# Attention and MLP in one instruction order: filler ordered by a clock, one exponential for two heads, fp32 maxima, and ScalarE for half of the second MLP product

## The chip, the cores and the metric

The kernel runs on one core of a Trainium2 chip. The metric is the device time in microseconds of one execution. The profile is of one execution of its own, with its own time. Engines: PE is TensorE's matmul and PEld its weight load, DVE is VectorE, ACT is ScalarE, POOL is GpSimd, SP is SyncE, which issues all DMAs here.

## The reference

```python
def _A_ref(x, wqkv, wo):              # 32 heads of 20, window of 256
    qkv = (x @ wqkv).reshape(B, S, 3, H, Dh).transpose(2, 0, 3, 1, 4)
    q, k, v = qkv[0], qkv[1], qkv[2]
    scores = jnp.einsum("bhqd,bhkd->bhqk", q, k) * (Dh ** -0.5)
    mask = (idx[:, None] - idx[None, :] >= 0) & (idx[:, None] - idx[None, :] < W)
    p = _softmax(jnp.where(mask[None, None], scores, -1e9), axis=-1)
    o = jnp.einsum("bhqk,bhkd->bhqd", p, v)
    return o.transpose(0, 2, 1, 3).reshape(B, S, D) @ wo
def _B_ref(x, w1, b1, w2, b2):
    h = jnp.einsum("bsd,df->bsf", x, w1) + b1
    r = jnp.where(h > 0, h, 0)
    return jnp.einsum("bsf,fd->bsd", r * r, w2) + b2
xn = _layernorm(A_x)
return A_x + _A_ref(xn, A_wqkv, A_wo) * _silu(_B_ref(xn, B_w1, B_b1, B_w2, B_b2))
```

x is 2048 x 640, wqkv 640 x 1920, w1 640 x 1536, w2 1536 x 640, wo 640 x 640, all fp32.

## The kernel before

Every fp32 operand of a product is split into a high part, rounded to the format in which PE multiplies, and a low part that is the rest; a product is high by high, high by low and low by high, summed in PSUM. So what leaves PSUM for a further product is copied by ACT (the high part) and subtracted by DVE or POOL (the low part).

**Before the loop** x is normalized, transposed and split (`transpose_chunks`, `split`, L111 to L113), the first q and k groups and all of v are computed, and q, k and v are stored in DRAM.

**The loop** (from L1149 on) has 268 steps: 16 pairs of heads by 16 query tiles, and 12 steps of lag. In step s:

- `scores` (L485): the scores of query tile q against its three key tiles, one matmul per head, into tile `sps`. `maxima` (L497) is a DVE reduction per head that adds the mask and takes the row maximum (`junk`, `mt`, L503). After four query tiles DVE splits the maxima into two bf16 parts (`mp`, L507 and L508).
- `scores_t` (L535), 9 steps behind: the transposed scores of key tile kb against three query tiles, with two more rows of `qs` that hold the negated maxima, into `stps`. `exps` (L546) is one ACT exponential per head (L549), and POOL zeroes the masked ends (L550, L552).
- `max_rows` (L511), in every fourth step: PE transposes the split maxima (L520) into the unused last quarter of the `sps` banks, DVE copies them to `mrow` (L526), and two DMAs bring them into the rows of `qs`.
- `high` (L555) and `low` (L560): the exponentials as two fp16 parts, by ACT (L557) and DVE (L563).
- `values` (L570), in every second step: 24 pairs of matmuls by v (tile `ops`); `normed` divides by the sums.
- `fill`: a generator, `filler` (L873), yields after each matmul of the other products: the remaining q and k groups (`qkps`), then eight MLP blocks (two halves of the hidden layer by four token blocks; `hps`, then `yps`), then the output projection. `fill` runs it until an amount of estimated PE time is used up: 35% of a step's share ahead of `high` and `low`, the rest behind, with a swing of 0.3 us between odd and even steps.

**Halves.** A product's matmuls are cut into the upper and the lower 64 rows of the array, which run side by side. `half` (L479) issues one at L481; the front half of a job runs ahead, the back half is put between later front halves, by two clocks, `clock[0]` and `clock[1]`, that add up the costs in `COST`. L481 is therefore the line of all of `qkps`, `hps`, `yps` and `ops`.

**Banks.** PSUM has 3 banks for the filler's products (`Acc`, L659), 2 for `sps`, 2 for `stps`, 1 for `ops`. An `Acc` takes the bank that was freed first, in program order; PE then waits for that bank's last reader.

**Evacuations.** When a job's back half is done, its evacuation is put into `pending`, and `soon` emits it once the clock is 0.3 us further (`SOON`); `flush` in the middle of each step emits all. For `hps`, `part` (L949 to L957) takes half of a bank: ACT's relu and square, DVE's `sq`, POOL's low part; the second half comes later, from the list `late`. For `yps` (L990) DVE adds b2 (first half of the hidden layer) or the stored first sum `yin` (second half), and `ysb` goes to DRAM.

**Weights** come in pieces: a DMA to `raw`, then ACT's high and DVE's low part (L812, L815), handed out by `tick` in the middle of a step.

All engines run in the order in which the program emits (`manual_schedule`); the semaphores are put in by the framework. Behind the loop, `out_filler` transposes the attention's output (`otp`), multiplies by wo (`wops`) and joins the two branches.

Of the kernel before, what the change touches and what calls it, by code (L numbers as in the profile page):

```python
# [16 lines left out]
P = 128  # L17
# [22 lines left out]
EARLY_FILL = 0.35  # L40
SWING = 0.3
# [9 lines left out]
SOON = 0.3  # L51
# [7 lines left out]
def attn_mlp_kernel(ctx: ExitStack, tc, x, wqkv, wo, w1, b1, w2, b2, out):  # L59
# [5 lines left out]
    pat = ctx.enter_context(tc.tile_pool(name="pat", bufs=2, space=PSUM))  # L65
    po_ = ctx.enter_context(tc.tile_pool(name="po", bufs=1, space=PSUM))
    turn = [0]
# [24 lines left out]
    identb = const.tile([P, P], BF16, name="identb")  # L92
    nc.gpsimd.tensor_copy(identb, ident)
# [5 lines left out]
    mps = [const.tile([P, P], BF16, name=f"mp{i}") for i in range(2)]  # L99
    for t_ in mps:  # L100
        nc.gpsimd.memset(t_, 0.0)
# [35 lines left out]
    with tc.tile_pool(name="ph1v", bufs=2) as p1v, tc.tile_pool(name="ph1", bufs=2) as p1, tc.tile_pool(name="ph1x", bufs=4) as p1b, tc.tile_pool(name="ph1w", bufs=1) as p1w:  # L137
# [34 lines left out]
        def transpose_chunks(b, xns):  # L172
            for c in range(KC):
                ps = mm_bank([P, BT], "tps") if c % 3 == 0 else pat.tile([P, BT], F32, tag=("s", "st")[c % 3 - 1], name="tps")
# [100 lines left out]
        with tc.manual_schedule(engines={E_.PE, E_.Activation, E_.DVE, E_.Pool, E_.SP}):  # L275
# [30 lines left out]
            def turned(t):  # L306
                nc.vector.reciprocal(rstd[:, t:t + 1], rstd[:, t:t + 1])
                xn = normalize(xts[0][t], mv[:, t, :], rstd[:, t:t + 1])
                r = []
                for c0, c1 in ((0, 4), (4, 5)):  # L310
                    ps = mm_bank([P, c1 - c0, P], "tps") if c0 == 0 else pat.tile([P, c1 - c0, P], F32, tag="s", name="tps")
# [17 lines left out]
            def first_group(w):  # L329
                firsts.append((w, 0, pat.tile([P, BT // 2], F32, tag="st", name="qkps"), 0, BT // 2))  # L330
                qk_group(*firsts[-1])
# [34 lines left out]
            for w in "kq":  # L366
                ps = pat.tile([P, BT // 2], F32, tag="s", name="qkps")
                seconds.append((w, 0, ps, BT // 2, BT // 2))
                qk_group(*seconds[-1])
# [113 lines left out]
    mts = {}  # L483

    def scores(p, q):  # L485
        i = p % 2
        k0 = max(0, q - 2)
        nk = (q - k0 + 1) * P
        r = [pat.tile([P, 4 * P], F32, tag="s", name="sps") for _ in range(2)]

        def one(hh):
            o = slice(hh * HP, hh * HP + KR)
            nc.tensor.matmul(r[hh][:, :nk], qs[i][o, q * P:(q + 1) * P], ks[i][o, k0 * P:k0 * P + nk], start=True, stop=True)  # L493
        both(lambda: one(0), lambda: one(1), COST[nk])
        return r, nk

    def maxima(p, q, r, nk):  # L497
        if q % 4 == 0:
            mts[p, q // 4] = at2.tile([P, 2, 4], F32, tag="mt", name="mt")
        mt = mts[p, q // 4]  # L500
        for hh in range(2):
            junk = at2.tile([P, 3 * P], BF16, tag="junk", name="junk")
            nc.vector.tensor_tensor_reduce(out=junk[:, :nk], in0=r[hh][:, :nk], in1=mask[:, 3 * P - nk:], scale=1.0, scalar=-3.0e38, op0=ALU.add, op1=ALU.max, accum_out=mt[:, hh, q % 4:q % 4 + 1])  # L503
        if q % 4 == 3:

            mp = mps[q // 4 % 2][:, 0:16].rearrange("p (h a b) -> p h a b", h=2, a=2)
            nc.vector.tensor_scalar(mp[:, :, 0, :], mt, -1.0, None, ALU.mult)  # L507
            nc.vector.scalar_tensor_tensor(mp[:, :, 1, :], mt, -1.0, mp[:, :, 0, :], ALU.mult, ALU.subtract)  # L508
            mts[p, q // 4] = mps[q // 4 % 2]

    def max_rows(p, g, tps=None):  # L511
        i = p % 2
        mp = mts.pop((p, g))
        if tps is None:
            tps = [pat.tile([P, 4 * P], F32, tag="s", name="mtp") for _ in range(2)]
        tps = [t_[:, 3 * P:3 * P + HP // 2].bitcast(BF16) for t_ in tps]

        def one(j):
            r = slice(j * HP, (j + 1) * HP)
            nc.tensor.transpose(tps[j], mp[r, :], identb[r, r])  # L520
        both(lambda: one(0), lambda: one(1), COST[61])

        def rest():
            mrow = at2.tile([16, P], F32R, tag="mrow", name="mrow")
            for j in range(2):
                nc.vector.tensor_copy(mrow[:, j * HP:(j + 1) * HP], tps[j][0:16, :])  # L526
# [8 lines left out]
    def scores_t(p, kb):  # L535
        i = p % 2
        n = min(3, NT - kb) * P
        r = [pat.tile([P, 3 * P], F32, tag="st", name="stps") for _ in range(2)]

        def one(hh):  # L540
            o = slice(hh * HP, hh * HP + KR + 2)
            nc.tensor.matmul(r[hh][:, :n], ks[i][o, kb * P:(kb + 1) * P], qs[i][o, kb * P:kb * P + n], start=True, stop=True)  # L542
        both(lambda: one(0), lambda: one(1), COST[n])
        return r, n

    def exps(p, kb, r, n):  # L546
        p32 = at2.tile([P, 2, 3 * P], F32, tag="p32", bufs=3, name="p32")
        for hh in range(2):
            nc.scalar.activation(p32[:, hh, :n], r[hh][:, :n], AF.Exp, scale=SCALE, bias=ebias)  # L549
# [82 lines left out]
    ended = deque()  # L632
    halved = [0.0]

    def soon():
        now = clock[0]
        if late and now >= halved[0] + 2 * SOON:
            flush(flushed[0])
        if ended and now >= ended[0][1] + SOON:
            flush(ended.popleft()[0])  # L640

    def flush(upto=None):
        halved[0] = clock[0]
# [13 lines left out]
    banks = [0, 1, 2]  # L657

    class Acc:  # L659

        def __init__(self, n, name):
# [211 lines left out]
    def filler():  # L873
# [5 lines left out]
        for g, b in order_qk:  # L879
# [9 lines left out]
            for w in "qk":  # L889
                hi, lo = (t() for t in ws[g][w])  # L890
                ps = Acc(BT, "qkps")

                def evac(ps=ps, w=w, g=g, b=b):
# [4 lines left out]
                    ps.free()  # L898
# [20 lines left out]
        for n, (hf, b) in enumerate(blocks):  # L919
# [11 lines left out]
            hs, whole, nxt = {}, set(), []  # L931
# [8 lines left out]
            for th in range(2):  # L940
                for fp in range(NFH // 2):
                    ps = Acc(BT, "hps")

                    def evac(ps=ps, th=th, fp=fp, fi=hf * NFH + 2 * fp, hs=hs, whole=whole):
# [31 lines left out]
            for tt in range(4):  # L976
# [4 lines left out]
                def start(nh, hf=hf, t=t, place=place, idx=4 * (n - NB) + tt, end=n == NB - 1 and tt == 3, n=n, tt=tt):  # L981
# [3 lines left out]
                    def evac():  # L985
# [4 lines left out]
                        nc.vector.tensor_add(ysb[:, sl], ps.tile, (yins[t] if hf else b2t)[:, sl])  # L990
                        ps.free()
# [21 lines left out]
                for nh in range(2):  # L1013
                    job = start(nh)
# [12 lines left out]
        ensure("o")  # L1027
        yield from out_filler(wo_part)
# [3 lines left out]
    def ready(u):  # L1032
        return state[2] >= NP * NT - NT + 4 * (u // 2) + 3 + LAG + 5
# [25 lines left out]
    def out_filler(wo_part):  # L1059
# [6 lines left out]
        def transposes(u):  # L1066
            ob = ld[u][0]
            big = bigp.tile([P, KC * BT], F32R, tag="big", name=f"oT_{u}")
            oT[u] = big.rearrange("p (s c n) -> p s c n", s=2, c=KC)
            for c0 in range(0, KC, 2):  # L1070
# [4 lines left out]
                else:  # L1075
                    ps = pat.tile([P, len(cs), MT], F32, tag="st" if c0 == 2 else "s", name="otp")
# [48 lines left out]

    fl = filler()
# [14 lines left out]
    per = total / (steps - 1)  # L1141
    with tc.manual_schedule(engines={E_.PE, E_.Activation, E_.DVE, E_.Pool, E_.SP}):
# [6 lines left out]
        for s in range(steps):  # L1149
# [17 lines left out]
            rows = between = None  # L1167
            if s % 4 == 0 and 0 < s <= NP * NT:
                def between(tps=None, s=s):
                    return max_rows((s - 1) // NT, (s - 1) % NT // 4, tps)  # L1170
# [4 lines left out]
            if between:  # L1175
                rows = between(sc[0] if a else None)
            if a:
                maxima(*a, *sc)
# [4 lines left out]
            if b:  # L1183
                exs[b] = (exps(*b, *stp), stp[1])
            fill(EARLY_FILL * per)
# [52 lines left out]
```

## Time and profile before

| | us |
|---|---|
| median of 3 runs (lowest to highest) | 956.03 (954.85 to 958.91) |
| the profiled execution | 955.41 |
| its span, first to last instruction | 953.7 |
| mean granted TensorE clock | 0.991 |

The page gives busy shares of the span; a busy PE isn't PE at its peak, since two halves may run side by side or one alone. A row of a group has its line, engine, operation, tiles (out<-in), shape and count, then busy us and mean ns of one, then the idle time of the engine just before and what ended it. A row of waits has us in total, times and the longest.

### The profile page before, as it was taken

What the parts mean: (1) busy time and instruction counts of PE and PEld (TensorE: products, weight loads), DVE (VectorE), ACT (ScalarE), POOL (GpSimd) and SP (SyncE); (2) the same over time, 40 slices, a digit from 0 to 9 for tenths busy, and PEclk for the clock granted to TensorE, in tenths of its full rate; (3) what the DMA queues carried; (4) which work ended last, traced back from release to release, by engine and by line L of the source; (5) the groups of instructions that cost most, each with busy time, mean ns of one, the idle gap of its engine ahead of it and who ended that gap; (6) DMA issues with size and microseconds to landing.
All of it is one profiled execution on the core that took longest, in us unless ns stands there. A gap on an engine that the chain in (4) does not pass through costs nothing.

```text
span 953.7 us, 35554 instructions
## 1 busy us (share of the span) xinstructions
PE 898.4 (94%) x14368; PEld 850.3 (89%) x14368; DVE 757.3 (79%) x2085; ACT 648.0 (68%) x1240; POOL 507.4 (53%) x800
## 2 busy tenths in 40 slices
PE   8999999999999989999999889889989989989998
PEld 8999989998888889889899879789889989888998
DVE  7774378998999988878888889978888878864564
ACT  4444347887778967867968867967877967873231
POOL 5010004665556866766867756856776856761000
PEclk9999999999999999999999999999999999999999
DMA  7997788787686262354355244465265274054773
GB/s 250 285 399 276 233 258 255 223 253 252 202 262 193 70 208 85 75 195 112 80 187 147 73 139 121 112 190 151 73 195 156 52 221 124 10 191 142 268 284 126
DMA packets 106108, 169.95 MB, mean 178 GB/s; under 512 B 42072, under 2 KB 59608, under 8 KB 103384
## 3 DMA queue, kind: packets, MB, share of 16 engines
q1 hardware_dynamic: 105944, 167.68, 56.1%
q8 instruction: 113, 1.85, 0.9%
q14 instruction: 51, 0.42, 0.2%
HBM read 96.15 MB, written 70.91 MB: 175 GB/s over the span
## 4 chain that ended last, share of the span: by engine, by line
PE 59%; DVE 20%; ACT 12%; issue 6%; POOL 3%; DMA 0%; DVEq 0%; ACTq 0%; POOLq 0%
PE yps L481 14%; PE ops L481 8%; PE wops L654 7%; PE vps L232 7%; PE qkps L481 6%; DVE junk L503 6%; DVE pl L563 5%; ACT p L549 5%; PE hps L481 5%; PE sps L493 4%; DVE sq L956 3%; PE qkps L209 3%; PE stps L542 3%; ACT relu L953 2%; ACT ph L557 2%
## 5 line engine op out<-in xcount | busy, mean ns | idle before, releaser
L549 ACT ACTIVATE p<-stps,ebias 128x384 f32<-128x384 f32 (+2 forms) x512 | 258.5, 557 | 140.7 <-PE stps L542 62.2
L481 PE MATMUL yps<-w,hh 64*128 64x320 f32 x1536 | 256.9, 320 | 35.1 <-DVE sq L956 24.1
L503 DVE CUSTOM_DVE_ANT_0 junk<-sps,mask 128x384 bf16<-128x384 f32 (+2 forms) x512 | 250.3, 525 | 46.9 <-PE sps L493 30.0
L550 POOL TENSOR_SCALAR_AFFINE_SELECT p<-p 128x256 f32<-128x256 f32 x256 | 151.0, 590 | 234.4 <-ACT p L549 160.6
L563 DVE TENSOR_TENSOR pl<-p,ph 128x768 f16<-128x768 f32 (+2 forms) x256 | 247.8, 968 | 3.5 <-ACT p L549 2.3
L481 PE MATMUL hps<-xb,w 64*128 64x256 f32 x2520 | 236.5, 285 | 2.5 <-DVE ysb L990 2.5
L481 PEld LDWEIGHTS yps<-w,hh 64*128 64x128 f32 x1536 | 197.8, 190 | 43.9 <-DVE sq L956 27.8
L481 PEld LDWEIGHTS hps<-xb,w 64*128 64x128 f32 x2520 | 221.1, 187 | 4.1 <-DVE ysb L990 4.1
L557 ACT ACTIVATE ph<-p 128x768 f16<-128x768 f32 (+2 forms) x256 | 205.7, 804 | 0.0
L481 PE MATMUL ops<-vp,ph 64*128 64x61 bf16 x2880 | 203.8, 190 | 0.1
L481 PE MATMUL ops<-vp,pl 64*128 64x61 bf16 x2880 | 201.7, 189 | 0.0
L481 PE MATMUL yps<-w,hl 64*128 64x320 f32 x768 | 193.4, 320 | 0.0
L481 PEld LDWEIGHTS <-pl 64*128 64x128 f16 x2880 | 177.1, 94 | 0.1
L481 PEld LDWEIGHTS <-ph 64*128 64x128 f16 x2880 | 174.4, 94 | 2.2 <-PE stps L542 0.6
L552 POOL TENSOR_SCALAR_AFFINE_SELECT p<-p 128x256 f32<-128x256 f32 x224 | 133.6, 596 | 0.0
L493 PE MATMUL sps<-ks,qs 60*128 60x384 f32 (+2 forms) x512 | 124.7, 366 | 8.4 <-DVE mrow L526 3.7
L481 PEld LDWEIGHTS yps<-w,hl 64*128 64x128 f32 x768 | 122.9, 189 | 0.0
L542 PE MATMUL stps<-qs,ks 62*128 62x384 f32 (+2 forms) x512 | 110.7, 344 | 0.3 <-DMA qs<-mrow 0.2
L481 PE MATMUL qkps<-xT,wgkh 64*128 64x512 f32 x320 | 103.8, 400 | 0.0
L957 POOL TENSOR_TENSOR hl<-sq,hh 128x256 fp32r<-128x256 f32 x96 | 88.2, 925 | 29.0 <-DVE sq L956 23.5
L481 PE MATMUL qkps<-xT,wgqh 64*128 64x512 f32 x320 | 103.2, 399 | 0.0
L493 PEld LDWEIGHTS sps<-ks,qs 60*128 60x128 f32 x512 | 69.0, 187 | 24.3 <-DVE mt L503 15.3
(110 smaller groups left out, 1627.0 us busy)
## 6 DMA issues: line engine op xcount, KB each, us to landing
ks<-k_d SPq DMA_DIRECT2D x64, 240.0 KB
qs<-q_d SPq DMA_DIRECT2D x64, 240.0 KB
xb<-xs SPq DMA_DIRECT2D x12, 1280.0 KB
xs<-xT SPq DMA_DIRECT2D x8, 1280.0 KB
y<-ysb SPq DMA_DIRECT2D x32, 320.0 KB
k_d<-shm SPq DMA_DIRECT2D x19, 512.0 KB
q_d<-shm SPq DMA_DIRECT2D x19, 512.0 KB
v_d<-vt SPq DMA_DIRECT2D x8, 976.0 KB
```

The lines of the kernel that those rows point to most:

```text
L232: nc.tensor.matmul(ps, xT[xp][b][:, c * BT + t * P: c * BT + (t + 1) * P], wv[wp][:, c, nh * HALF:(nh + 1) * HALF], start=first and m == 0 ...
L481: return nc.tensor.matmul(out, a[r], b_[r], skip_group_check=True, **kw)
L493: nc.tensor.matmul(r[hh][:, :nk], qs[i][o, q * P:(q + 1) * P], ks[i][o, k0 * P:k0 * P + nk], start=True, stop=True)
L503: nc.vector.tensor_tensor_reduce(out=junk[:, :nk], in0=r[hh][:, :nk], in1=mask[:, 3 * P - nk:], scale=1.0, scalar=-3.0e38, op0=ALU.add, op ...
L542: nc.tensor.matmul(r[hh][:, :n], ks[i][o, kb * P:(kb + 1) * P], qs[i][o, kb * P:kb * P + n], start=True, stop=True)
L549: nc.scalar.activation(p32[:, hh, :n], r[hh][:, :n], AF.Exp, scale=SCALE, bias=ebias)
L550: nc.gpsimd.affine_select(p32[:, :, 0:P], p32[:, :, 0:P], pattern=[[0, 2], [1, P]], compare_op=ALU.is_ge, fill=0.0, base=0, channel_multip ...
L552: nc.gpsimd.affine_select(p32[:, :, 2 * P:], p32[:, :, 2 * P:], pattern=[[0, 2], [-1, P]], compare_op=ALU.is_gt, fill=0.0, base=0, channel ...
L557: nc.scalar.activation(ph[:, :, :n], p32[:, :, :n], AF.Copy)
L563: nc.vector.tensor_sub(pl[:, :, :n], p32[:, :, :n], ph[:, :, :n])
L654: nc.tensor.matmul(ps, a, b_, start=j == 0, stop=j == n - 1)
L957: nc.gpsimd.tensor_sub(hh[1][:, sl], sq, f32(hh[0][:, sl]))
```

## The change

- **Order by a clock.** `fill` runs until `clock[0]` reaches a target: 40% of a step's `pace` ahead of `high` and `low`, the whole at the step's end, less the cost of `values` where it follows. `pace` is the estimated PE time of all products and the attention's matmuls, by the step. `banks` holds with each bank the time at which it is expected free: 2.0 us after a q or k evacuation is emitted, 1.6 us after an MLP one. `room` yields the rest of the slot unless a bank is expected within `PATIENCE`, 0.5 us; a second product that lacks its input does the same. An evacuation is emitted as soon as its job is done, with the DMAs that are due ahead of it.
- **One exponential.** `sps` and `stps` become one tile of two banks each, and one ACT instruction takes both heads.
- **Maxima.** They stay fp32 in one tile `mt`, PE transposes them as fp32, and the split is made on the way out of PSUM: ACT the negated high part, DVE the rest. Four DMAs, one per head and part, in place of two.
- **b2.** In the first half of the hidden layer ACT copies `yps` out and nothing is added; b2 is added when the stored sum is read back for the output, by one DVE instruction on 128x1280 for each of eight pieces. The loads for the output begin a step later.

```diff
-EARLY_FILL = 0.35
-SWING = 0.3
+EARLY_FILL = 0.4
-SOON = 0.3
+SOON = 0.4
+PATIENCE = 0.5
...
+    spair, tpair = (pat.tile([P, 2, BT], F32, tag=t_, name=t_) for t_ in ("sps", "stps"))
+    turn, swap = [0], [0, 0]
+
+    def at_bank(k, n):
+        swap[k] ^= 1
+        return (spair, tpair)[k][:, swap[k], :n]
...
+            m = 32 * (q // 4 % 2) + 4 * hh + q % 4
+            nc.vector.tensor_tensor_reduce(out=junk[:, :nk], in0=spair[:, hh, :nk], in1=mask[:, 3 * P - nk:], scale=1.0, scalar=-3.0e38, op0=ALU.add, op1=ALU.max, accum_out=mt[:, m:m + 1])
+
+    def max_rows(p, g):
...
-            nc.tensor.transpose(tps[j], mp[r, :], identb[r, r])
-        both(lambda: one(0), lambda: one(1), COST[61])
+            nc.tensor.transpose(spair[:, j, 3 * P:3 * P + HP], mt[r, :], ident[r, r])
+        both(lambda: one(0), lambda: one(1), COST[P])
...
-            mrow = at2.tile([16, P], F32R, tag="mrow", name="mrow")
-            for j in range(2):
-                nc.vector.tensor_copy(mrow[:, j * HP:(j + 1) * HP], tps[j][0:16, :])
+            m = slice(32 * (g % 2), 32 * (g % 2) + 8)
+            mrow = at2.tile([40, 2, P], F32R, tag="mrow", bufs=1, name="mrow")[m]
+            hi, lo = (mrow[:, a, :].rearrange("m (j n) -> m j n", j=2) for a in range(2))
+            src = spair[m, :, 3 * P:3 * P + HP]
+            nc.scalar.activation(hi, src, AF.Copy, scale=-1.0)
+            nc.vector.scalar_tensor_tensor(lo, src, -1.0, f32(hi), ALU.mult, ALU.subtract)
             for hh in range(2):
-                o = hh * HP + KR
-                post(f32(qs[i])[o:o + 2, g * 512:(g + 1) * 512].rearrange("o (a n) -> o a n", a=4), f32(mrow)[8 * hh:8 * hh + 8, :])
+                for a in range(2):
+                    o = hh * HP + KR + a
+                    post(f32(qs[i])[o:o + 1, g * 512:(g + 1) * 512].rearrange("r (q n) -> r q n", q=4), f32(mrow)[4 * hh:4 * hh + 4, a, :])
...
-        for hh in range(2):
-            nc.scalar.activation(p32[:, hh, :n], r[hh][:, :n], AF.Exp, scale=SCALE, bias=ebias)
+        nc.scalar.activation(p32[:, :, :n], tpair[:, :, :n], AF.Exp, scale=SCALE, bias=ebias)
...
     def soon():
-        now = clock[0]
-        if late and now >= halved[0] + 2 * SOON:
+        if late and clock[0] >= halved[0] + SOON:
             flush(flushed[0])
-        if ended and now >= ended[0][1] + SOON:
-            flush(ended.popleft()[0])
...
-    banks = [0, 1, 2]
+    banks = [(0.0, j) for j in range(3)]
+
+    def room():
+        while state[2] < 10 ** 6 and not (banks and banks[0][0] < clock[0] + PATIENCE):
+            yield None
...
-            self.bank, self.n = banks.pop(0), n
+            (at_, self.bank), self.n = banks.pop(0), n
+            clock[0] = max(clock[0], at_)
...
-        def free(self):
-            banks.append(self.bank)
+        def free(self, after):
+            banks.append((clock[0] + after, self.bank))
+            banks.sort()
...
         def done():
-            pending.append(evac)
-            ended.append((mark(), clock[1]))
+            if state[2] < 10 ** 6:
+                flush()
+                post_all()
+                evac()
+            else:
+                pending.append(evac)
...
+                yield from room()
                 ps = Acc(BT, "qkps")
...
-                    ps.free()
+                    ps.free(2.0)
...
+                    yield from room()
                     ps = Acc(BT, "hps")
...
-                            whole.add((th, fp))
-                            ps.free()
+                            made.add((th, fp))
+                            ps.free(1.6)
                         late.append(rest)
+                        halved[0] = clock[0]
...
-                        nc.vector.tensor_add(ysb[:, sl], ps.tile, (yins[t] if hf else b2t)[:, sl])
-                        ps.free()
+                        if hf:
+                            nc.vector.tensor_add(ysb[:, sl], ps.tile, yins[t][:, sl])
+                        else:
+                            nc.scalar.activation(ysb[:, sl], ps.tile, AF.Copy)
+                        ps.free(1.6)
...
-                    while (tt // 2, fc // 2) not in whole:
-                        if pending or late:
+                    while (tt // 2, fc // 2) not in made:
+                        if state[2] < 10 ** 6:
+                            yield None
+                        elif pending or late:
                             flush()
-                            yield None
...
-        return state[2] >= NP * NT - NT + 4 * (u // 2) + 3 + LAG + 5
+        return state[2] >= NP * NT - NT + 4 * (u // 2) + 3 + LAG + 6
...
-            ob = ld[u][0]
+            ob, yb = ld[u]
+            nc.vector.tensor_add(yb, yb, b2t.unsqueeze(1).to_broadcast([P, 2, D]))
...
-    total = 8 * (KC - 1) * 15 * 0.213 + 2 * NB * (6 * 15 * 0.213 + 8 * 18 * 0.133)
     steps = NP * NT + LAG + 3
-
-    def fill(amount):
-        state[1] += amount
-        while state[0] < state[1]:
+    pace = (8 * (KC - 1) * 15 * COST[BT] + 4 * NB * (3 * 30 * COST[MT] + 4 * 18 * COST[HALF]) + NP * (2 * NT * COST[3 * P] + 12 * NT * COST[61])) / (steps - 1)
+
+    def fill(upto):
+        while clock[0] < upto:
             c = next(fl, None)
             if c is None:
-                state[1] = state[0]
+                clock[0] = upto
                 return
-            state[0] += c
+            if whole[0]:
+                clock[:2] = [clock[0] + c] * 2
...
-            fill(EARLY_FILL * per)
+            fill((s + EARLY_FILL) * pace)
...
-            fill((1 - EARLY_FILL) * per + SWING * (-1) ** (s - LAG - 3))
             if e and e[1] % 2:
+                fill((s + 1) * pace - 24 * COST[61])
                 values(*e)
+            else:
+                fill((s + 1) * pace)
```

More of the change, by code (lines that the diff above doesn't have):

```diff
@@ L366, in attn_mlp_kernel @@
             for w in "kq":
-                ps = pat.tile([P, BT // 2], F32, tag="s", name="qkps")
+                ps = at_bank(0, BT // 2)
                 seconds.append((w, 0, ps, BT // 2, BT // 2))
@@ L488, in scores @@
         nk = (q - k0 + 1) * P
-        r = [pat.tile([P, 4 * P], F32, tag="s", name="sps") for _ in range(2)]
         def one(hh):
             o = slice(hh * HP, hh * HP + KR)
-            nc.tensor.matmul(r[hh][:, :nk], qs[i][o, q * P:(q + 1) * P], ks[i][o, k0 * P:k0 * P + nk], start=True, stop=True)
+            nc.tensor.matmul(spair[:, hh, :nk], qs[i][o, q * P:(q + 1) * P], ks[i][o, k0 * P:k0 * P + nk], start=True, stop=True)
         both(lambda: one(0), lambda: one(1), COST[nk])
-        return r, nk
@@ L497, in maxima @@
[L497 to L500, printed above, removed]
+        return nk
+    def maxima(p, q, nk):
         for hh in range(2):
             junk = at2.tile([P, 3 * P], BF16, tag="junk", name="junk")
[L503 to L509, printed above, removed]
@@ L1013, in filler @@
                 for nh in range(2):
+                    yield from room()
                     job = start(nh)
@@ L1075, in transposes @@
                 else:
-                    ps = pat.tile([P, len(cs), MT], F32, tag="st" if c0 == 2 else "s", name="otp")
+                    ps = at_bank(c0 == 2, len(cs) * MT).rearrange("p (c n) -> p c n", n=MT)
                 for c in cs:
@@ L1166, in attn_mlp_kernel @@
                     load_v(p + 1)
[L1167 to L1170, printed above, removed]
+            rows = None
             if a:
@@ L1174, in attn_mlp_kernel @@
                 stp = scores_t(*b)
-            if between:
-                rows = between(sc[0] if a else None)
+            if s % 4 == 0 and 0 < s <= NP * NT:
+                rows = max_rows((s - 1) // NT, (s - 1) % NT // 4)
             if a:
-                maxima(*a, *sc)
+                maxima(*a, sc)
             if rows:
```

40 lines of the change are left out of this document (14 added, 26 removed).

## The prediction

> **What bounds the kernel now.** I read four views in this order: the page's busy shares and its chain of work that ended last, then busy time by stage, then who waited for whom, then one stall in the timeline.
>
> ```profile
> PE 898.4 (94%) x14368; PEld 850.3 (89%) x14368; DVE 757.3 (79%) x2085; ACT 648.0 (68%) x1240; POOL 507.4 (53%) x800
> ...
> PE 59%; DVE 20%; ACT 12%; issue 6%; POOL 3%; DMA 0%; DVEq 0%; ACTq 0%; POOLq 0%
> ```
>
> TensorE is busy nearly always, and yet the chain lies on it for 59% only: a third of the time something else decides. The stages tell where (columns: length, then busy time of PE, PEld, DVE, ACT, POOL, then the granted clock, DMA share and GB/s).
>
> ```profile
> 118.00:303.70 185.70, 182.51 (x2708) 165.75 (x2709) 165.85 (x481) 140.26 (x254) 96.80 (x161) 1.00 0.78 243
> 303.70:868.00 564.30, 519.65 (x10313) 494.10 (x10309) 475.16 (x1351) 436.04 (x841) 389.78 (x605) 0.98 0.44 127
> 868.00:953.70 85.70, 81.02 (x606) 80.10 (x604) 44.60 (x89) 22.03 (x34) 1.50 (x3) 1.00 0.63 216
> 506.00:526.70 20.70, 20.67 (x465) 20.21 (x460) 17.88 (x54) 18.44 (x37) 17.31 (x27) 1.00 0.40 109
> 526.70:555.00 28.30, 22.51 (x415) 21.19 (x411) 23.66 (x65) 21.39 (x43) 17.65 (x29) 0.94 0.34 89
> ```
>
> The loop of 268 steps runs from 118 to 868 us: 750 us, 2.80 a step. In its first part (the q and k products) PE hardly rests. In its second (the MLP blocks) PE idles 564.3 - 519.65 = 44.7 us. The last two rows are eight steps each, counted by their pairs of sps matmuls: the first eight take 20.7 us (2.59 a step) with PE never idle, the next eight 28.3 us with PE idle for 5.8. So the steps have a clean pace of 2.59, and stretches that fall off it.
>
> ```profile
> PE yps L481 <- DVE sq L956: 24.1, 15, 2.6
> PE yps L481 <- DVE ysb L990: 10.6, 15, 2.2
> PE sps L493 <- DVE mrow L526: 3.7, 8, 0.7
> PE sps L493 <- DVE mt L503: 3.2, 9, 1.1
> PE hps L481 <- DVE ysb L990: 2.5, 5, 0.9
> ```
>
> The rows give total us, times and the longest. 24.1 + 10.6 + 2.5 = 37.2 us of the idle time are the first matmul of an MLP accumulation that waits for a DVE reader to empty one of the three mm banks. One of them, in the timeline:
>
> ```profile
> 549.50 1.12 DVE L563 TENSOR_TENSOR pl<-p,ph 128x768 f16<-128x768 f32 x1
> 550.55 1.22 DVE L815 TENSOR_TENSOR w<-raw,w 128x512 fp32r<-128x512 f32 x2
> 551.70 0.48 DVE L990 TENSOR_TENSOR ysb<-yps,b2t 128x320 f32<-128x320 f32 x1
> 552.23 0.42 PE L481 MATMUL yps<-w,hh 64*128 64x320 f32 x1 [2.19 <-DVE ysb L990]
> 553.19 1.05 ACT L549 ACTIVATE p<-stps,ebias 128x384 f32<-128x384 f32 x2 [2.39 <-PE stps L542]
> ```
>
> DVE does a low half of the weights before the copy that frees the bank, PE stands for 2.19 us, and behind that matmul in PE's queue wait the next step's scores, for which ACT stands 2.39 us. No engine is full here: one order of instructions holds three of them. Then the clock:
>
> ```profile
> 400.00:425.00 25.00, 22.02 (x394) 20.63 (x391) 19.47 (x62) 16.74 (x32) 16.67 (x27) 0.93 0.59 191
> ...
> 825.00:850.00 25.00, 21.67 (x397) 20.56 (x392) 17.51 (x33) 20.28 (x38) 18.75 (x31) 0.93 0.22 61
> ```
>
> Five stretches of 25 us in the loop are granted 0.93, of which these are the first and the last (the others begin at 525, 550 and 625); the rest have 1.00. Each of the five has such a stall in it or just before: 5 x 25 x 0.07 = 8.7 us lost.
>
> **The change part by part.**
>
> *The order by a clock.* A product now starts only if its own clock expects a bank within 0.5 us; otherwise the filler gives up the rest of its slot and the attention matmuls come next in PE's queue. The evacuation is put in the queues of ACT and DVE as the group's last matmul is emitted, where before it stood 0.3 us of that clock behind. Giving up a slot costs PE nothing by itself, as its queue holds no pause: the work moves to a later step, at worst behind the last one. So the 37.2 us can go. They go where the guess (a bank is free 1.6 or 2.0 us after its evacuation is queued) covers DVE's backlog; above, the copy itself took 0.48 us and stood behind 2.2 us of other work, more than the guess. I take two thirds: **-24.8** (bounds 0 and -37.2). The clock follows, two thirds of 8.7: **-5.8** (0 to -8.7).
>
> The Trainium skill, "TensorE: Matmul & The Clock Gate", section "Why this matters for your kernels", has the rate fall only after idle gaps of over about 3 us. No wait above is longer than 2.6 us, so by that rule these dips aren't the stalls' doing, the term is 0 and the sum 923; its section "A second HAM failure mode: psum-queue depth-cycling" does allow for many short ones.
>
> *DVE's load.* Rows, with busy us and mean ns:
>
> ```profile
> L508 DVE SCALAR_TENSOR_TENSOR mp<-mt,mp 128x8 bf16<-128x8 f32 x64 | 13.4, 210 | 2.2
> L507 DVE TENSOR_SCALAR mp<-mt 128x8 bf16<-128x8 f32 x64 | 13.1, 205 | 2.2
> L526 DVE CAST mrow<-sps 16x64 fp32r<-16x64 bf16 x126 | 21.3, 204 | 0.0
> L503 DVE CUSTOM_DVE_ANT_0 junk<-sps,mask 128x128 bf16<-128x128 f32 x32 | 7.9, 283 | 2.6 <-PE sps L520 2.2
> L990 DVE TENSOR_TENSOR ysb<-yps,b2t 128x320 f32<-128x320 f32 x32 | 15.2, 476 | 0.2 <-PE yps L481 0.2
> L563 DVE TENSOR_TENSOR pl<-p,ph 128x768 f16<-128x768 f32 x224 | 227.5, 1015 | 3.0 <-ACT p L549 2.3 <-PE stps L542 0.5 <-ACT ph L557 0.2
> ```
>
> Gone are the two operations that split the maxima, both casts out of PSUM and the 32 additions of b2: 13.4 + 13.1 + 21.3 + 15.2 = 63.0 us. New is one subtraction of 8x128 out of PSUM for each of 64 groups, not in the trace; bounds are the cast's 204 ns and, for two operands of 128 elements, 283; I take 283, the nearer form: 18.1 us. DVE sheds 44.9 us in the loop. It is the limiter only where the chain says so, 20% of the span: **-9** (0 if it is elsewhere, -45 if DVE decided all through).
>
> *ACT.*
>
> ```profile
> L549 ACT ACTIVATE p<-stps,ebias 128x384 f32<-128x384 f32 x448 | 235.2, 578 | 119.2 <-PE stps L542 55.4 <-DVE pl L563 33.2 <-PE sps L520 25.7
> L549 ACT ACTIVATE p<-stps,ebias 128x128 f32<-128x128 f32 x32 | 10.0, 363 | 12.8 <-DVE pl L563 6.3 <-PE sps L520 5.3 <-PE ops L481 0.7
> L557 ACT ACTIVATE ph<-p 128x768 f16<-128x768 f32 x224 | 189.1, 844 | 0.0
> L256 ACT ACTIVATE vt<-vps 128x320 bf16<-128x320 f32 x32 | 14.5, 452 | 41.0 <-PE vps L232 38.7 <-DMA v_d<-vt 2.2
> ```
>
> Back to back an exponential takes 235.2 / 448 = 0.525 us, a pair 1.05. The line through 363 ns at 128 elements and 578 at 384 gives 0.90 at 768 (low bound 0.84, the copy of that size; high 1.05): 0.15 saved in each of 256 steps, 38 us. Back come 32 copies of 128x320 at 0.453 (14.5 us), and 64 copies of 8x128 out of PSUM, which the trace doesn't have: 0.36 by the 128-element exponential, bounds 0.20 (the smallest cast above, on DVE) and 0.58: 23 us. Net nothing: **0** (-16 to +11 in busy time, of which 12% is on the chain). The new wait: the negated maxima stand before the exponential in ACT's queue and wait for the transposes, which PE issues right behind the stps pair that the exponential waits for anyway. So PE's two short matmuls hide it; without that cover it would be 64 x 0.2 = 13 us on the exponentials, the high copies behind them and POOL.
>
> The Trainium skill, "ScalarE: Activation LUTs", section "Rules for kernel authors", speaks against the moved copies: plain arithmetic belongs on VectorE, up to three times as fast in bf16. This trace differs for the fp32 PSUM form, 452 ns on ACT against 476 on DVE. At three times 476 the copies would cost 31 us more of ACT, at its share of 12% +4, and the sum 921.
>
> *PE's transposes and the rows.*
>
> ```profile
> L520 PE MATMUL sps<-identb,mp 64*128 64x64 bf16 x126 | 14.0, 203 | 0.4
> ...
> 876.19 1.09 PE otp L1079 x10
> ...
> PEld L520 <- DVE mp L508: 4.0, 13, 0.8
> ...
> L623 SPq DMA_DIRECT2D qs<-mrow x128: 610/617/711, 129.3 to 832.9; - x128
> ...
> PE stps L542 <- DMA qs<-mrow: 0.2, 1, 0.2
> ```
>
> An fp32 transposition of 128 columns takes 0.109 us in the chain, one of 64 about half. In place of the bf16 pair I take +0.03 for each of 64: **+2** (0 to 64 x 0.109 = +7). The transposition no longer waits for the split maxima, 4.0 us of waits of which PE's pipeline hid some: **-2** (0 to -4). The rows go to qs in four DMAs in place of two. SP issues one in 0.62 us, so the last leaves 1.2 us later; behind it on SP stand weights, stores and the blocks' loads. The scores that need the rows come three steps (3 x 2.59 = 7.8 us) later and have waited once for 0.2 us: **0** (to +13, 0.2 for each group, if the slack is used up).
>
> *The tail.* b2 is added to 128x1280 in eight pieces: by 1015 ns for 768 elements 1.69 us each, 13.5 in all. DVE is busy for 44.6 of 85.7 us there, PE for 81.0, so all but the first lie beside PE. The first lies beside the first transposes and ACT's copy: **+1** (0 to +13.5).
>
> *Sum:* -24.8 - 5.8 - 9 - 2 + 2 + 1 = -38.6. The profiled execution took 955.41 (a span of 953.7 and 1.7 around it), 0.6 under the median of 956.03. Forecast 955.4 - 38.6 = **916.8**.
>
> **The rivals.**
>
> 1. All stalls go: every step runs at 2.59. 268 x 2.59 = 694 in place of 750, so 955.4 - 56 = 899. For it: the clean eight steps, with DVE busy for 17.88 of 20.70, show that the pace can be held through a product stage. Against: the first part is near DVE's limit (165.85 of 185.7) without any bank wait.
> 2. The stalls move: the clock that orders doesn't know DVE's backlog, so the banks still come late, or the scores wait for DVE's maxima (6.9 us now) in place of the products. Then only the lighter DVE counts: 955.4 - 9 - 2 + 3 = 947. For it: the 2.2 us of other work ahead of the copy above.
> 3. The clock dips have another cause: 916.8 + 5.8 = 923.
> 4. Slower: evacuations queued too early. ACT and DVE take their queues in order; a copy that stands ahead of its group's last matmul holds the high and low copies behind it, then `pts`, then the values on PE. There are 32 + 64 + 2 x 48 = 192 pieces. If each waits the 0.3 us that the old order allowed, 58 us come back: 916.8 + 58 = 975. It decides from 38.6 / 192 = 0.20 us a piece. For it: ACT's exponentials already wait 55.4 us for PE's stps (their row above), so ACT does run up to PE's front. Against: that is at the head of a step; inside a step, as in the stall shown, the copies come late because ACT and DVE are behind.
> 5. It does not do what it says: the clock's order comes out like the old one, and the time with it, 955.
>
> **How the numbers follow.** Forecast (900 to 936) 0.48; all stalls go (885 to 900) 0.15; the clock's other cause 0.05 (inside the first one's span); the stalls move (940 to 950) 0.12; no difference 0.06; slower 0.14. About 0.5% (4.8 us) is what a measurement of this kernel can tell from no change. Faster: 0.48 + 0.15 + 0.05 + 0.12 = 0.80; within: 0.06; slower: 0.14. A range of 888 to 958 leaves out the slower case, and the end of the first rival, about 0.2 together.
>
> **What would show it.** Right: yps's waits for DVE fall from 34.7 us to under 15; no stretch of the loop under a granted clock of 1.00 but one or two; 256 exponentials at about 0.9 us; DVE's busy time near 757 - 45 + 13 = 725, ACT's near 648. Wrong: PE's idle time in the loop unchanged with other releasers (rival 2); ACT's and DVE's waits for qkps, hps and yps grown by tens of us (rival 4); MLP products behind the last step, with the tail longer than 86 us; stps waiting for mrow's DMA.

## The result and the profile after

The changed kernel takes 971.05 us in the median (969.47 to 972.08, 4 runs), the kernel before 955.44 (954.65 to 958.91) beside it: a ratio of 1.0155, 95% interval 1.0126 to 1.0184. It is slower, by 1.6%; the forecast was 916.8, and the range ended at 958. Of one kernel below, the order with joined sps, the profiled execution took 1670 us where the four others took 940 to 942; it is left out, so that kernel has no stage times.

The page of the changed kernel, busy shares and chain, then its busy time by stage. The loop counts here from the first sps matmul to the last yps matmul; before, that was from 118.0 to 867.0 us.

```profile
PE 901.1 (93%) x14368; PEld 847.7 (87%) x14368; DVE 730.9 (75%) x1869; ACT 633.9 (65%) x1080; POOL 485.8 (50%) x798
...
PE 61%; ACT 13%; DVE 12%; issue 7%; DMA 3%; POOL 2%; SPq 1%; DVEq 0%; ACTq 0%; POOLq 0%
```

```profile
0.00:121.00 121.00, 114.97 (x754) 109.60 (x754) 71.22 (x165) 49.97 (x112) 19.04 (x30) 1.00 0.82 285
121.00:303.70 182.70, 173.21 (x2468) 153.51 (x2469) 149.84 (x396) 124.08 (x194) 76.21 (x143) 1.00 0.75 241
303.70:866.20 562.50, 525.40 (x10497) 499.94 (x10493) 452.64 (x1208) 436.90 (x740) 388.57 (x622) 0.99 0.44 130
866.20:969.40 103.20, 87.54 (x656) 84.68 (x656) 57.20 (x101) 22.99 (x35) 1.96 (x4) 0.96 0.51 180
```

No engine has clearly more to do (PE's busy time is 901.1 us for 898.4), and the kernel is slower. DVE's busy time fell by 26 us and ACT's by 14, but the loop is 745.2 us where it was 749.0, and PE idles in it for 46.6 us where it idled for 47.3. Ahead of it 3.0 us are lost (121.0 for 118.0), behind it 16.5 (103.2 for 86.7). The five longest of PE's waits in the changed kernel (total us, times, the longest):

```profile
PE sps L492 <- DVE mt L500: 25.2, 39, 2.6
PE yps L483 <- DVE sq L952: 9.0, 8, 1.9
PE sps L1083 <- DVE oT L115: 8.6, 6, 1.5
PE sps L492 <- DVE mrow L516: 5.9, 15, 0.7
PE sps L178 <- DVE xT L115: 3.5, 3, 1.6
```

The waits of yps, 34.7 us before, fell to 11.6 with the smaller rows, as forecast, and hps waits no more. In their place sps waits for the maxima 25.2 us, where it was 3.2. Two rows are new: transposes into the sps tile that wait for DVE, three ahead of the loop (L178) and six in the tail (L1083).

What the forecast had called hidden stands in ACT's rows. First the groups, then one fourth step in the timelines of PE, ACT and DVE:

```profile
L538 ACT ACTIVATE p<-stps,ebias 128x768 f32<-128x768 f32 (+2 forms) x256 | 218.8, 855 | 59.1 <-PE stps L532 29.1 <-DVE pl L552 24.6 <-PE ops L483 1.7
L515 ACT ACTIVATE mrow<-sps 8x128 fp32r<-8x128 f32 x64 | 17.1, 268 | 95.8 <-PE ops L483 38.8 <-PE yps L483 16.8 <-DVE mt L500 12.2
```

```profile
587.40 0.28 PE L532 MATMUL stps<-qs,ks 62*128 62x128 f32 x2
587.47 0.28 PE L507 MATMUL sps<-ident,mt 64*128 64x64 f32 x2
```

```profile
587.77 0.42 ACT L950 ACTIVATE hh<-relu 128x256 fp32r<-128x256 f32 x1
589.29 0.27 ACT L515 ACTIVATE mrow<-sps 8x128 fp32r<-8x128 f32 x1 [1.10 <-DVE mt L500]
589.58 0.48 ACT L538 ACTIVATE p<-stps,ebias 128x256 f32<-128x256 f32 x1
```

```profile
588.17 0.55 DVE L500 CUSTOM_DVE_ANT_0 junk<-sps,mask 128x384 bf16<-128x384 f32 x1
588.64 0.08 DVE L500 DVE_READ_ACCUMULATOR2_ANT mt<- 128x1 f32 x1
588.64 0.55 DVE L500 CUSTOM_DVE_ANT_0 junk<-sps,mask 128x384 bf16<-128x384 f32 x1
589.12 0.08 DVE L500 DVE_READ_ACCUMULATOR2_ANT mt<- 128x1 f32 x1
```

PE's transposes are done by 587.75. ACT is free at 588.19. The copy of the maxima's rows starts at 589.29, when DVE has just ended this step's own maxima (589.20), which it reads from other columns of the same banks. The exponential, whose stps were there at 587.7, starts at 589.58. ACT idles 95.8 us before the 64 copies, 1.5 us each, part of it for the transposes. The page puts most of that down to PE, since a wait for several semaphores goes to the last event seen; the program's list of waits for this instruction names both DVE and PE.

### The profile page after: what moved, and what is told of

It is laid out like the page before. It is cut to its first block, busy times and chain, and to the rows that moved or that the text cites. A ratio compares the mean times of both kernels' runs of the same rounds, so it can differ in the third digit from the quotient of the medians.

```text
span 969.4 us, 35471 instructions
## 1 busy us (share of the span) xinstructions
PE 901.1 (93%) x14368; PEld 847.7 (87%) x14368; DVE 730.9 (75%) x1869; ACT 633.9 (65%) x1080; POOL 485.8 (50%) x798
## 4 chain that ended last, share of the span: by engine, by line
PE 61%; ACT 13%; DVE 12%; issue 7%; DMA 3%; POOL 2%; SPq 1%; DVEq 0%; ACTq 0%; POOLq 0%
PE yps L483 14%; PE ops L483 9%; PE wops L638 8%; PE vps L234 7%; PE qkps L483 6%; PE hps L483 5%; ACT p L538 5%; PE sps L492 4%; DVE junk L500 4%; PE stps L532 3%; ACT relu L949 2%; DVE pl L552 2%; ACT ph L546 2%; PE qkps L211 2%; DVE sq L952 2%
## 5 line engine op out<-in xcount | busy, mean ns | idle before, releaser
L539 POOL TENSOR_SCALAR_AFFINE_SELECT p<-p 128x256 f32<-128x256 f32 x256 | 162.8, 636 | 257.5 <-ACT p L538 211.2
L483 PE MATMUL yps<-w,hh 64*128 64x320 f32 x1536 | 249.3, 315 | 11.6 <-DVE sq L952 9.0
L538 ACT ACTIVATE p<-stps,ebias 128x768 f32<-128x768 f32 (+2 forms) x256 | 218.8, 855 | 59.1 <-PE stps L532 29.1
L552 DVE TENSOR_TENSOR pl<-p,ph 128x768 f16<-128x768 f32 (+2 forms) x256 | 243.6, 952 | 6.8 <-PE ops L483 4.7
L483 PE MATMUL hps<-xb,w 64*128 64x256 f32 x2520 | 232.8, 285 | 0.0
L483 PE MATMUL yps<-w,hl 64*128 64x320 f32 x768 | 187.5, 313 | 0.0
L492 PE MATMUL sps<-ks,qs 60*128 60x384 f32 (+2 forms) x512 | 108.5, 381 | 32.4 <-DVE mt L500 25.2
L541 POOL TENSOR_SCALAR_AFFINE_SELECT p<-p 128x256 f32<-128x256 f32 x224 | 112.3, 501 | 0.0
L492 PEld LDWEIGHTS sps<-ks,qs 60*128 60x128 f32 x512 | 56.8, 186 | 54.5 <-DVE mt L500 38.3
L532 PE MATMUL stps<-qs,ks 62*128 62x384 f32 (+2 forms) x512 | 99.3, 351 | 1.9 <-ACT p L538 1.3
L953 POOL TENSOR_TENSOR hl<-sq,hh 128x256 fp32r<-128x256 f32 x96 | 82.5, 863 | 31.1 <-DVE sq L952 30.1
```

Of the source, the lines that this page charges most:

```text
L483: return nc.tensor.matmul(out, a[r], b_[r], skip_group_check=True, **kw)
L492: nc.tensor.matmul(spair[:, hh, :nk], qs[i][o, q * P:(q + 1) * P], ks[i][o, k0 * P:k0 * P + nk], start=True, stop=True)
L532: nc.tensor.matmul(tpair[:, hh, :n], ks[i][o, kb * P:(kb + 1) * P], qs[i][o, kb * P:kb * P + n], start=True, stop=True)
L538: nc.scalar.activation(p32[:, :, :n], tpair[:, :, :n], AF.Exp, scale=SCALE, bias=ebias)
L539: nc.gpsimd.affine_select(p32[:, :, 0:P], p32[:, :, 0:P], pattern=[[0, 2], [1, P]], compare_op=ALU.is_ge, fill=0.0, base=0, channel_multip ...
L541: nc.gpsimd.affine_select(p32[:, :, 2 * P:], p32[:, :, 2 * P:], pattern=[[0, 2], [-1, P]], compare_op=ALU.is_gt, fill=0.0, base=0, channel ...
```

## The experiments

Theory W: ACT's small copy waits for DVE's maxima of the same step, as accesses to one bank are put in order, and holds the exponential behind it. Rivals: J, a joined tile makes PE wait for both of its banks; M, the stall that left yps came back at sps because DVE is late; B, the addition of b2 in the tail. The expectations below name three more: X, the one long exponential holds both stps banks; R, the small copy is held in ACT's queue by PE's transposes; T, the fp32 transposes or the four DMAs. W was formed only after the first two groups of runs.

After the changed kernel itself, the runs were made in three groups (up to "all but the order", up to "joined sps", and the rest), with the kernel before beside each: 955.5, 955.2 and 957.4 us. So a difference in us between two groups can be off by some 2 us; the ratios are free of that.

| kernel | us | ratio to before, 95% interval | ahead, loop, tail |
|---|---|---|---|
| changed | 971.1 | 1.0155 (1.0126 to 1.0184) | 121.0, 745.2, 103.2 |
| changed, sps apart | 953.8 | 0.9975 (0.9955 to 0.9995) | 116.7, 743.9, 92.1 |
| changed, b2 as before | 971.6 | 1.0169 (1.0151 to 1.0187) | 121.0, 745.8, 103.2 |
| order alone | 929.3 | 0.9724 (0.9696 to 0.9752) | 116.5, 716.2, 94.2 |
| all but the order | 998.8 | 1.0445 (1.0417 to 1.0472) | 121.0, 777.2, 98.5 |
| order + one exponential | 916.9 | 0.9603 (0.9574 to 0.9632) | 116.5, 705.1, 94.0 |
| order + fp32 maxima | 968.2 | 1.0136 (1.0105 to 1.0166) | 116.5, 759.5, 90.6 |
| order + ACT's copies | 931.0 | 0.9747 (0.9716 to 0.9778) | 116.6, 716.6, 97.3 |
| order + joined sps | 941.1 | 0.9855 (0.9821 to 0.9890) | - |
| order + fp32 maxima, rows on DVE | 933.1 | 0.9747 (0.9715 to 0.9779) | 116.5, 723.6, 92.0 |
| order + one exp. + fp32 maxima, rows on DVE | 924.1 | 0.9661 (0.9628 to 0.9693) | 116.5, 711.6, 93.4 |
| changed, rows on DVE | 932.1 | 0.9741 (0.9713 to 0.9769) | 121.2, 706.6, 102.1 |
| changed, rows ahead of maxima | 930.7 | 0.9723 (0.9693 to 0.9753) | 121.2, 705.6, 100.5 |

**sps as two tiles.**

```diff
-    spair, tpair = (pat.tile([P, 2, BT], F32, tag=t_, name=t_) for t_ in ("sps", "stps"))
+    spair = [pat.tile([P, BT], F32, tag=f"sps{i}", name="sps") for i in range(2)]
+    tpair = pat.tile([P, 2, BT], F32, tag="stps", name="stps")
...
```

> The changed kernel with sps as two tiles of one bank each (stps stays one tile of two); the maxima's copies out of PSUM become one small one per bank on ACT and on DVE. Theory J (the joined tile): a wait put in for one bank of a joined tile also covers the other bank. Then the waits of sps for DVE's mt in the loop (25.2 us on PE) fall to about the 3.2 us of before, the three gaps of 0.9 to 1.6 us ahead of the loop and the 1.4 us gaps in each unit of the tail go: 971 - 3 - 11 - 20 = about 937. Rival M (the stall moved): sps waits in the loop because DVE's maxima are late whatever the tiles are; only the gaps ahead of and behind the loop go: about 957. Rival B (the addition of b2 in the tail): tail unchanged, about 967.

953.8, near M's 957. Of the 17.3 us that went, the stages show 4.3 ahead of the loop, 11.1 in the tail and 1.3 in the loop. The gaps at L178 and L1083 are gone. Of sps's waits in the loop this is left, 9.7 us where it was 25.2:

```profile
PE sps L493 <- DVE mt L501: 9.7, 15, 2.1
```

The loop hardly noticed: theory J holds outside the loop and fell inside it. The changed kernel's 25.2 us of sps waiting for mt were a symptom, not the price.

**b2 back.** Of the ACT copy and the addition in the tail, both undone:

```diff
-                        if hf:
-                            nc.vector.tensor_add(ysb[:, sl], ps.tile, yins[t][:, sl])
-                        else:
-                            nc.scalar.activation(ysb[:, sl], ps.tile, AF.Copy)
+                        nc.vector.tensor_add(ysb[:, sl], ps.tile, (yins[t] if hf else b2t)[:, sl])
...
-            nc.vector.tensor_add(yb, yb, b2t.unsqueeze(1).to_broadcast([P, 2, D]))
```

> The changed kernel with b2 added by DVE as yps is evacuated, as before, and no addition in the tail. Rival B: the eight additions of 1.49 us are what makes the tail 14 us longer: about 958. Theory J: they lie beside PE, and the tail keeps its gaps at sps: 971, or 1 to 3 more for 15 us more of DVE in the loop.

971.6, stages the same: B fell. The additions take 1.48 us each, and PE's work covers them.

**The order alone, and all but the order.** The first is the kernel before with `room`, the timed `banks`, `pace`, the immediate evacuation and their constants; the second the kernel before with the rest of the diff.

> The kernel before with the clock's order alone; tiles, exponentials, maxima and b2 as before. Theory J: without the joined tile the order brings what it takes from the waits of yps, about 25 us, less what DVE's higher load costs: 930 to 940, with sps waiting for mt for under 8 us. Rival M: the stall comes back at sps (20 us or more on PE), about 950 to 956. Either way the tail is as long as before, about 86 us.

> The kernel before in its old order, with everything else of the change (joined tiles, one exponential, fp32 maxima, ACT's copies, b2 in the tail). Theory J: the joined tile costs by itself: sps waits for mt in the loop rise to about 20 us, and ahead of and behind the loop 14 us are lost: 975 to 985, since the waits of yps stay. Rival M: in the loop nothing is lost and DVE's lighter load gains about 9: about 960.

The order alone gives 929.3, 26 us faster, slightly better than J's 930 to 940. Its waits (PE, longest first):

```profile
PE yps L481 <- DVE sq L963: 8.8, 10, 2.1
PE sps L493 <- DVE mrow L526: 6.4, 11, 1.4
PE sps L493 <- DVE mt L503: 4.6, 11, 0.8
...
PE yps L481 <- DVE ysb L998: 1.4, 3, 0.6
```

34.7 us of yps's waits became 10.2; sps waits 11.0 where it waited 6.9, so 4 of the 24 us came back there. M holds for a sixth. The tail, expected at 86 us, is 94.2, but only because it is counted from the last yps matmul: 20 us of the attention's steps still follow that one, where 5 us did before. From the last product by v (ops) to the end it is 74.0 us for 81.7. The rest alone costs 43 us, beyond what either theory expected (960 to 985). So the loss lay in the parts forecast as neutral or light, and these were tried singly on the order.

**One exponential, fp32 maxima, ACT's copies, joined sps**, each added to the order alone:

```diff
 # one exponential
-            nc.scalar.activation(p32[:, hh, :n], r[hh][:, :n], AF.Exp, scale=SCALE, bias=ebias)
+        nc.scalar.activation(p32[:, :, :n], tpair[:, :, :n], AF.Exp, scale=SCALE, bias=ebias)
...
 # fp32 maxima, one pair of copies for each of the two banks
+            for j in range(2):
+                nc.scalar.activation(hi[:, j], spair[j][m, 3 * P:3 * P + HP], AF.Copy, scale=-1.0)
+            for j in range(2):
+                nc.vector.scalar_tensor_tensor(lo[:, j], spair[j][m, 3 * P:3 * P + HP], -1.0, f32(hi[:, j]), ALU.mult, ALU.subtract)
...
 # joined sps
+    spair = pat.tile([P, 2, BT], F32, tag="sps", bufs=1, name="sps")
...
```

> The order alone (929.3 us), with stps as one tile of two banks and one exponential for both heads; sps, maxima and b2 as before. Of the 24.5 us between the order alone and the change with sps apart, theory X puts most on this: the next step's stps of either head must wait until the one long exponential has read both banks, where before the first head's bank came free half an exponential earlier: 945 to 950. Rival R (the maxima's copy in ACT's queue costs it): ACT does 38 us less, and the time is 925 to 932.

> The order alone, with the fp32 maxima: transposed as fp32, split out of PSUM by ACT and DVE (one small copy per bank), four DMAs. sps and stps are tiles of one bank each, two exponentials, b2 as before. Rival R: the small copies stand in ACT's queue ahead of the exponentials and wait there for PE's transposes, and sps of the next step waits for the pair of ACT and DVE: 940 to 950. Theory X: 929 to 934.

> The order alone, with ACT's copies of the first half's yps and b2 added in the tail. The change with b2 put back showed no difference (971.6 to 971.0); if that holds here too: 927 to 932. If DVE's 15 us in the loop had been hidden there by the other stalls, 920 to 925; if the additions in the tail had, 935 to 942.

> The order alone, with nothing but sps made one tile of two banks: same instructions, same buffers. Theory J, tested alone: 929.3 + 17 = about 946, with the gaps of the changed kernel ahead of the loop (three, 3.5 us together) and in the tail (six, 8.6 us), and sps waiting longer for mt. If waits go by bank and not by tile: 929.

916.9, 968.2, 931.0 and 941.1. Theory X fell: the one exponential (with stps as one tile) brings 12.4 us, more than its rival gave. The fp32 maxima cost 38.9 us, more than R's 21 at the most. ACT's copies change nothing that can be told. Joining sps costs 11.8. The four differences and the order's 929.3 sum to 969.3, where the whole change measured 971.1, so little is left between the parts.

The group of the small copies in the order with fp32 maxima shows whom they wait for:

```profile
L516 ACT ACTIVATE mrow<-sps 8x64 fp32r<-8x64 f32 x128 | 27.3, 214 | 83.9 <-DVE mt L501 80.9 <-PE hps L484 1.0 <-DMA ks<-k_d 0.6
```

Of 83.9 us of ACT's idle time 80.9 end with DVE's maxima. With that, theory W had a price, and rival T (the fp32 transposes or the four DMAs) was to be told from it.

**The rows' copy on DVE, or ahead of the maxima.** The first edit is in three kernels (in the two with sps apart, one copy for each bank), the second in the changed one:

```diff
 # rows on DVE
-            nc.scalar.activation(hi, src, AF.Copy, scale=-1.0)
+            nc.vector.tensor_scalar(hi, src, -1.0, None, ALU.mult)
 # rows ahead of maxima
+            if rows:
+                rows()
             if a:
                 maxima(*a, sc)
-            if rows:
-                rows()
```

> The order with fp32 maxima (968.2 us), where the negated high part of the maxima is copied out of PSUM by DVE in place of ACT; nothing else differs. Theory W: ACT's copy had to wait until DVE had read the maxima out of the same bank in this step (80.9 us of such waits), with the exponentials behind it in ACT's queue; on DVE, which is in order anyway, that wait is gone, and the time falls to the order's own, 929 to 935. Rival T: the fp32 transposes or the four DMAs cost it: still 955 or more.

> The order, one exponential, sps apart, fp32 maxima split by DVE alone, b2 as before. By theory W the fp32 maxima then cost nothing and save DVE about 0.2 us in each of 64 groups: 910 to 918, at or under the order with one exponential and bf16 maxima (916.9). By rival T: 945 or more.

> The changed kernel (971.1 us) with that one instruction moved from ACT to DVE. By theory W what is left against the best version is the joined sps (12 us by the run that had it alone): 925 to 938. By rival T: 960 or more.

> The changed kernel with the same instructions, in which the two copies of the maxima's rows are emitted ahead of this step's maxima in place of behind them. Theory W: ACT's copy then waits for PE's transposes alone and the exponential starts about 1 us sooner in every fourth step, while DVE's maxima wait some 0.5 us for the copies: 940 to 955. If the copy on ACT costs by itself, wherever it stands: 968 to 975.

933.1, 924.1, 932.1 and 930.7. T fell as the main cost: the fp32 transposes and the four DMAs are in all four kernels, and 35, 39 and 40 us went without touching them (968.2 to 933.1, 971.1 to 932.1 and to 930.7). The last is the plainest: the same instructions, one pair emitted a little sooner, and 971.1 becomes 930.7, better than the 940 to 955 expected. Its ACT rows:

```profile
L538 ACT ACTIVATE p<-stps,ebias 128x768 f32<-128x768 f32 (+2 forms) x256 | 219.6, 858 | 84.4 <-PE stps L532 38.3 <-DVE pl L552 36.0 <-DVE ysb L988 2.3
L515 ACT ACTIVATE mrow<-sps 8x128 fp32r<-8x128 f32 x64 | 17.0, 265 | 24.7 <-PE sps L507 22.3 <-DMA raw<-in_A_wqkv_dram 1.5 <-DMA q_d<-slo 0.3
```

The copy's idle time fell from 95.8 to 24.7 us, and what is left ends with the transposes (L507). The exponential's rose from 59.1 to 84.4, so ACT idles 45.8 us less before the two, and the kernel is 40.4 us faster. The lists of waits in the two programs say the same, for the same copy:

```
changed:               L515 ACTIVATE mrow<-sps 8x128 [waits 4 DMA, DVE, PE]
rows ahead of maxima:  L515 ACTIVATE mrow<-sps 8x128 [waits 4 DMA, PE]
```

Of the 64 copies, 63 name DVE in the changed kernel and 17 with the rows ahead. And sps still waits for mt, without harm:

```profile
PE sps L492 <- DVE mt L500: 19.7, 35, 1.8
```

924.1 missed its 910 to 918: on DVE, the fp32 split saves nothing against the bf16 one. Its two copies for each bank take 44.0 us where the bf16 split and its casts took 52.1, yet DVE is busy for 753.4 us, against 748.0 with one exponential and bf16 maxima (916.9), and the kernel is 7 us slower than that one (5.5 by the ratios). The other such pair, 933.1 against 929.3, can't be told apart by its ratios. What the fp32 maxima still cost without W, and whether it is T, stays open. The fastest version is the order with one exponential and otherwise the old kernel, at 916.9 (0.9603 of before). Its loop and its exponential:

```profile
116.50:821.60 705.10, 683.83 (x12911) 648.21 (x12910) 629.54 (x1825) 540.00 (x834) 486.63 (x761) 1.00 0.54 163
```

```profile
L552 ACT ACTIVATE p<-stps,ebias 128x768 f32<-128x768 f32 (+2 forms) x256 | 220.3, 860 | 134.8 <-DVE pl L566 59.0
```

PE idles for 21 us of 705, and the granted clock is 1.00.

## Why the prediction was wrong, step by step

- **The order by a clock and the clock it frees, -24.8 and -5.8: right together.** The run with the order alone has both terms in it and measured -26.2, against -30.6. yps's waits fell by 24.5 us, the two thirds that were named. Only 4 us of the waits moved to sps (rival 2), and evacuations queued at once did no harm (rival 4).
- **The clock, -5.8: its direction right.** The order alone has two stretches of lower clock in its loop for five, and with one exponential the loop has a granted clock of 1.00 (row above). The changed kernel still has three (0.93 each), more than the one or two that were forecast. Before, PE stood idle for 1.8 to 2.6 us just ahead of each of the five drops, so waits under 3 us do go with them. But not every one does: the order alone and the order with one exponential have the same longest wait of yps, 2.1 us, with two stretches and none. The rule of the Trainium skill, "TensorE: Matmul & The Clock Gate", section "Why this matters for your kernels" (idle gaps of over about 3 us), doesn't cover this trace. How many us the clock alone gave was not separated.
- **DVE's load, -9: wrong in size, as far as it was tried.** DVE's busy time fell as worked out (731 for 725). But b2 put back on DVE cost 0.6 us, and taking it off DVE in the order alone gained nothing (931.0 for 929.3). No run takes away the rest of the load by itself.
- **ACT, 0: the term mis-sized, by netting.** The sizes were right: a full exponential took 0.90 us, as estimated, and all of them together 220.3 us for 258.5. This brought 12.4 us. The likely reason is that it shortens the way from stps to the low half in each step; no run shows that apart. The 32 copies of yps that I had set against it cost 1.7 us at most, and the 64 small ones far more than their busy time (next point). So busy time saved and added on one engine did not cancel in the kernel's time. The rule that arithmetic belongs on VectorE ("ScalarE: Activation LUTs", "Rules for kernel authors", of the Trainium skill) was weighed on the yps copies, where it made no difference (427 ns on ACT, 480 on DVE). It pointed the right way for the rows' copy, but not for its reason: 268 ns on ACT were never the price.
- **The new wait in ACT's queue: the step that failed.** The prediction named the copy ahead of the exponential, said that it "wait[s] for the transposes", and that "PE's two short matmuls hide it". It priced the lack of cover at 13 us, with the transposes as the only releaser, and put the term at nothing. The copy also waited for DVE's two maxima of the step (1.0 us of DVE's time, in the same two banks) and whatever DVE still had ahead of them. Without that wait ACT idled 71 us less before the 64 copies, 1.1 us each, and the changed kernel was 39 to 40 us faster.
- **The joined tile: a term that was missing.** I took one tile of two banks for the same buffers as two tiles. Outside the loop its transposes into the other bank waited for the first bank's reader (3.5 and 8.6 us in PE's waits above): 4.3 us ahead of the loop and 11.1 in the tail by the run with sps apart, 11.8 in the run that had the joined tile alone. So the tail did come out longer than 86 us, a sign named for wrong, but not for the reason named there (MLP products behind the last step): the last yps matmul ends at 866.2 us, the last product by v at 878.2.
- **The sign of rival 2.** PE's idle time in the loop stayed, with sps in place of yps as the waiting product, which is what was to speak for rival 2. It misled: the run with sps apart took 15.5 us of that wait away and gained 1.3 us in the loop.
- **Transposes, DMAs, additions of b2 (+2, -2, 0, +1): small, as far as shown.** L507 took 217 ns for 203, an addition 1.48 us for 1.69, and PE's waits of stps for a row's DMA didn't appear. What the transposes and DMAs cost in all is no more than the 4 to 7 us by which the fp32 maxima are slower with the rows on DVE.

With the measured terms the forecast's own sum would have been 955.4 - 26.2 - 12.4 + 38.9 + 11.8 + 1.7 = 969.2. The slower case had a chance of 0.14, on another mechanism.

## What to carry to other kernels

When an operation is moved to another engine, write down every access to its operand's bank or tile that stands ahead of it in program order, not only the one that makes its data: on the engine that did those accesses the order was free, on another it is a wait, and everything in that engine's queue pays it. Where program order decides the waits, emit the small operation ahead of the large one in the same bank. Test the parts of a large change singly before netting them: here +39 and +12 hid -26 and -12.

## What was unexpected

Two reads of one PSUM bank, by ACT and by DVE, in different columns, were ordered one behind the other (80.9 us of ACT's idle time ended so). Whether the hardware needs that order was not tried; the wait is one that the framework puts in. And a wait of PE that grew from 3.2 to 25.2 us, the largest new row in the profile, cost next to nothing: at 19.7 us of it the kernel ran at 930.7.
